# A list-scheduling kernel gets a planner with free slots, a rule against certain DVE and POOL instructions side by side, and a PE-clock term

## The chip, the cores and the metric

One core of a Trainium2 chip. The time is device microseconds of one execution. In the first measurement the kernel before takes 195.49 us (median of 4 runs, 195.04 to 196.26). The profile is one execution with the hardware profiler on; its span, from first to last instruction, is about 1.7 us shorter than the time of that same run (before: 193.5 and 195.17; after: 186.7 and 188.42). PE is TensorE, DVE VectorE, ACT ScalarE, POOL GpSimd, SP SyncE.

## The reference

A transformer block on 2048 tokens of width 448, modulated by one conditioning row. Attention has 16 heads of 28 and looks at 8 keys, every second token back; the MLP has 1792 hidden units.

```python
mod = (silu(c) @ w_mod).reshape(1, 6, 1, -1)      # sa, ca, ga, sb, cb, gb
h = layernorm(x) * (1 + ca) + sa
x = x + ga * attention(h, wqkv, wo)               # 8 keys, step 2 back
h = layernorm(x) * (1 + cb) + sb
x = x + gb * (gelu(layernorm(h) @ w1 + b1) @ w2 + b2)
```

## The kernel before

The kernel first collects tasks (an engine, an estimated duration, what it reads and writes), then a planner simulates the engines and emits the tasks in the order found. That order is fixed: each engine works through its own queue, and semaphores do the rest. So the planner's estimates are not the run time, but they decide who stands behind whom.

```python
QKE = "ADAADAAD"        # which engine copies each of 8 q/k groups from PSUM: A = ACT, D = DVE
ROOM = {"L": 2, "S": 4, "et": 3, "den": 4, "zh": 6, "yT": 3, "hm": 3, "vb": 3}
...
    def ps_one(shape, name, dtype=FP32):
        return Buf("S", lambda: ps_s.tile(shape, dtype, name=name, tag="s1"), name)   # 4 tiles in rotation
...
    def plan(self):         # [...] rank = longest tail to the end; then, in simulated time:
                for t in ready[e]:
                    [...]   # ready, and enough free tiles in its rooms
                    if best is None or (t.rank, -t.n) > (best.rank, -best.n):
                        best = t
```

The work: normalize 16 tiles of 128 tokens (statistics, z, transpose on PE, hT), project q and k in eight groups for 256 or 512 tokens at a time (pq), project v, then 17 blocks of attention (lt scores, their exponentials et, mask on DVE, pd and po sums, division oT), output projection (pw), second normalization (z2, h2, y), a DMA transposition to yT, and the MLP (p1, GELU, p2). The profile drops digits, so p1 and p2 both appear as `p`. PSUM is in two rooms: two tiles of two banks (lt, p1) and four of one bank (everything else). ACT loads a table between exponentials and GELU (1.28 us in the trace), so the blocks come in four phases.

Of the kernel before, what the change touches and what calls it, by code (L numbers as in the profile page):

```python
# [8 lines left out]
FP32 = mybir.dt.float32  # L9
BF16 = mybir.dt.bfloat16  # L10
ACT = mybir.ActivationFunctionType
# [20 lines left out]
QKE = "ADAADAAD"  # L32
# [7 lines left out]
FILL_UNTIL, FILL_SHARE = 12.0, 0.85  # L40
ROOM = {"L": 2, "S": 4, "et": 3, "den": 4, "zh": 6, "yT": 3, "hm": 3, "vb": 3}
SEM = 0.07
# [3 lines left out]
class Buf:  # L46


    def __init__(self, room, make, name=""):
        self.room, self.make, self.name, self.users, self._t = room, make, name, [], None  # L50

    @property
    def t(self):
        if self._t is None:
            self._t = self.make()
        return self._t


class Task:
    def __init__(self, n, eng, us, fn, bufs, rank_add, late):  # L60
        self.n, self.eng, self.us, self.fn, self.bufs = n, eng, us, fn, bufs
        self.name = f"{eng} {fn.__qualname__.split('.')[-1]}:{fn.__code__.co_firstlineno}"
        self.rank_add, self.late = rank_add, late
        self.before, self.after = {}, []
        self.rank = 0.0
        self.fill = 0


class Planner:
# [6 lines left out]
    def add(self, eng, us, fn, reads=(), writes=(), bufs=(), after=(), order_after=(), rank_add=0.0, late=0.0):  # L76
        t = Task(len(self.tasks), eng, us, fn, bufs, rank_add, late)
        for k in list(reads) + [b for b in bufs]:
            if k in self.writer:
                self._edge(self.writer[k], t, True)  # L80
        for k in writes:
            if k in self.writer:
                self._edge(self.writer[k], t, True)
            for r in self.readers.get(k, ()):
                self._edge(r, t, True)
            self.writer[k], self.readers[k] = t, []
        for k in reads:
            self.readers.setdefault(k, []).append(t)
        for b in bufs:
            b.users.append(t)  # L90
        for a in after:
            self._edge(a, t, True)
        for a in order_after:
            self._edge(a, t, False)
        self.tasks.append(t)
        return t
# [14 lines left out]
    def plan(self):  # L111
        for t in reversed(self.tasks):
            tail = 0.0
            for a in t.after:
                lag = (DRAIN[t.eng] + SEM + t.late) if a.before[t] else 0.0
                tail = max(tail, a.rank + lag)
            t.rank = t.us + tail + t.rank_add
        left = {t: len(t.before) for t in self.tasks}
# [5 lines left out]
        room = {r: list(range(n)) for r, n in ROOM.items()}  # L124
        held, users_left = set(), {}
        for t in self.tasks:
            for b in t.bufs:
                users_left[b] = len(b.users)
        free_at = {e: 0.0 for e in DRAIN}
        freeing = []  # L130
        order = []
        now = 0.0
        while len(order) < len(self.tasks):
            for f in sorted(freeing, key=lambda f: f[0]):
                if f[0] <= now:
                    room[f[1]].append(f[2])
            freeing = [f for f in freeing if f[0] > now]
            started = False
            for e in ("PE", "DVE", "ACT", "POOL", "SP"):
                if free_at[e] > now:  # L140
                    continue
                best = None
                for t in ready[e]:
                    if ready_at[t] > now:
                        continue
                    need = {}
                    for b in t.bufs:
                        if b not in held:
                            need[b.room] = need.get(b.room, 0) + 1
                    if any(len(room[r]) < n for r, n in need.items()):  # L150
                        continue
                    if best is None or (t.rank, -t.n) > (best.rank, -best.n):
                        best = t
                if best is None:
                    continue
                t = best
                if e == "PE" and now < FILL_UNTIL:
                    t.fill = int(max(0.0, now - free_at[e]) * FILL_SHARE / (0.43 if now < 6.0 else 0.215))
# [4 lines left out]
                for b in t.bufs:  # L163
                    if b not in held:
                        held.add(b)
                        b.slot = room[b.room].pop(0)
                end = now + t.us
                free_at[e] = end
                done = end + DRAIN[e] + t.late
                for b in t.bufs:  # L170
                    users_left[b] -= 1
                    if users_left[b] == 0:
                        freeing.append((done + SEM, b.room, b.slot))
# [10 lines left out]
            times = [v for v in free_at.values() if v > now] + [f[0] for f in freeing if f[0] > now]  # L184
            times += [ready_at[t] for e in ready for t in ready[e] if ready_at[t] > now]
            if not times:
                raise RuntimeError("no task can start: " + repr(room) + repr(
                    [(b.room, b.name, [(u.n, u.name) for u in b.users if u not in order]) for b in held if users_left[b]]))
            now = min(times)
        self.order = order  # L190
        self.span = max(free_at.values())

    def emit(self):
        for t in self.order:
            if t.fill:
                self.filler(t.fill)
            t.fn()
# [3 lines left out]
def kernel(  # L201
# [24 lines left out]
    ps_l = ctx.enter_context(tc.tile_pool(name="ps_l", bufs=ROOM["L"], space=bass.MemoryType.PSUM))  # L226
    ps_s = ctx.enter_context(tc.tile_pool(name="ps_s", bufs=ROOM["S"], space=bass.MemoryType.PSUM))
    wk = ctx.enter_context(tc.tile_pool(name="wk", bufs=3))
    hbm = ctx.enter_context(tc.tile_pool(name="hbm", bufs=1, space=bass.MemoryType.DRAM))

    def ps_big(shape, name):
        return Buf("L", lambda: ps_l.tile(shape, FP32, name=name, tag="l2"), name)

    def ps_one(shape, name, dtype=FP32):
        return Buf("S", lambda: ps_s.tile(shape, dtype, name=name, tag="s1"), name)

    def sb(room, shape, dtype, name):
        return Buf(room, lambda: wk.tile(shape, dtype, name=name, tag=room, bufs=ROOM[room]), name)
# [82 lines left out]
    add("ACT", 0.4, lambda: nc.scalar.dma_start(out=c_row[:, 0:D], in_=c), writes=["c_row"], late=2.0, rank_add=500)  # L321
# [10 lines left out]
    zero(0.6, lambda: hT[z_row, KT - 1, :], ["hT0"])  # L332
    zero(0.15, lambda: Wv[z_row, KT - 1, :], ["Wv0"])
# [11 lines left out]
    gate = None  # L345
    for i in range(2):
        gate = zero(0.8, lambda i=i: wmod2[i].t[z_row, KT - 1, :], [f"wmod0{i}"], [wmod2[i]], "POOL", 600 - 200 * i, [gate] if gate else [])
    add("DVE", 0.3, lambda: nc.vector.memset(wo_s[:], 0.0), writes=["wo"], rank_add=400)
# [17 lines left out]
    def pool(us, fn, writes, reads=(), rank_add=300, gated=True):  # L366
        add("POOL", us, fn, writes=writes, reads=reads, rank_add=rank_add, order_after=[gate] if gated else [])
# [73 lines left out]
    def normalize(dst, src, mv, which, b, reads, writes, bufs=()):  # L441
# [3 lines left out]
                   reads=list(reads) + [f"mv{id(mv)}_{b}", f"rs{which}_{b}"], writes=writes, bufs=bufs)  # L445
# [36 lines left out]
    def evac_h(kt, ptr, k, c0, n, eng, bs):  # L482
        kw = KW[kt]
# [36 lines left out]
    def spread(half, k0, k1, eng):  # L520
# [10 lines left out]
        if eng == "DVE":  # L531
            add("DVE", 0.08 + 0.134 * (k1 - k0), lambda: nc.vector.tensor_copy(out=o, in_=i()), reads=reads, bufs=[wqk_st], writes=[f"W{half}{k0}"])
# [6 lines left out]
    def front_qk(bs, engs):  # L539
        n, c0 = 128 * len(bs), tok_col(bs[0])  # L540
        for m in range(8):
            pq = ps_one([128, n], "pq")

            def mm(m=m, pq=pq):
                for kt in range(KT):
# [4 lines left out]
                        reads=[f"W{m // 4}0", f"W{m // 4}{KT - 1}", "hT0"]  # L550
                        + [f"h{kt}_{b}" for kt in range(KT) for b in bs], bufs=[pq]), pq)
# [9 lines left out]
    def mods():  # L561
# [19 lines left out]
        for i in range(2):  # L581
# [3 lines left out]
                reads=["ga"] + [f"wo{r}" for r in range(4)], writes=[f"wos{i}"])  # L585
# [3 lines left out]
    def w2_scale():  # L589
        for i in range(FT // 2):  # L590
            add("DVE", 0.55, lambda i=i: nc.vector.tensor_tensor(
                out=w2_s[:, 2 * i:2 * i + 2, :], in0=w2_s[:, 2 * i:2 * i + 2, :],
                in1=gb_bc.unsqueeze(1).to_broadcast([128, 2, D]), op=ALU.mult), reads=["gb"] + [f"w2l{k}" for k in (2 * i // 7, (2 * i + 1) // 7)], writes=[f"w2_{i}"])
# [4 lines left out]
    def attention(b, tbl, prev_w1):  # L598
# [3 lines left out]
        vbuf = Buf("vb", lambda: vbufs[vbuf.slot], "vb")  # L602
# [7 lines left out]
        P.wrote(add("PE", 0.76, vmm, reads=["wva", "wvb", "Wv0", "hT0"] + PADK + [f"h{kt}_{t}" for kt in range(KT) for t in tb], bufs=[pv, vbuf]), pv)  # L610
# [14 lines left out]
        lm = add("PE", 0.45, lmm, reads=PADK + [f"{s}{ft}_{t}" for s in "qk" for ft in range(4) for t in tb],  # L625
# [3 lines left out]
        for half in range(2):  # L629
# [10 lines left out]
            add("DVE", 0.57, msk, bufs=[et], reads=["mask"], writes=[(et, half)])  # L640
# [13 lines left out]
        P.wrote(add("PE", 0.62, dmm, reads=[(et, 0), (et, 1), "ones"], bufs=[et, vbuf, pd, po]), pd, po)  # L654
# [25 lines left out]
    def out_proj(t):  # L680
# [12 lines left out]
        if bi == 0:  # L693
# [8 lines left out]
                    reads=["g2"], bufs=[z2, h2]), h2)  # L702
        P.wrote(add("DVE", 0.31, lambda: nc.vector.tensor_tensor(out=h2.t[:], in0=h2.t[:], in1=sb_bc, op=ALU.add),
                    reads=["sb"], bufs=[h2]), h2)
# [76 lines left out]
    for half, engs in enumerate(SPREAD):  # L781
        spread(half, 0, KT - 1, engs[0])
        spread(half, KT - 1, KT, engs[1])
    front_qk([0, 1], "AAADAAAD")
# [6 lines left out]
    for pi, (blocks, tiles) in enumerate(phases):  # L791
        exps.clear()
        lt_mms.clear()
        for b in blocks:
            attention(b, tbl, prev_w1)
            if b == 0:
                front_ln([4, 5, 6, 7], False)
                front_qk([4, 5, 6, 7], QKE)
                mods()
            if b == 2:  # L800
                front_ln([8, 9, 10, 11], False)
                front_qk([8, 9, 10, 11], QKE)
                w2_scale()
            if b == 4:
                front_ln([12, 13, 14, 15], False)
                front_qk([12, 13, 14, 15], QKE)
# [44 lines left out]
```

## Time and profile before

| | before |
|---|---|
| time, median of 4 | 195.49 us |
| span of the profiled run | 193.5 us |
| PE work at full clock, counted from dense stretches | 164.5 us |
| of it ahead of the first MLP matmul (51.31 us) | 31.4 us |
| DVE busy from 20 to 46.47 us | all of it |

To read it, do not take PE's 93% busy for 93% useful. The fillers at the start (useless matmuls that are meant to bring the clock up) count as busy, and so do matmuls at half clock (the clock records show 0.50 from 47.52 to 50.93 us). How the work is counted instead, and the lines, are in the prediction.

### The profile page before, as it was taken

The numbers are of one execution on the slowest core, as the hardware profiler recorded it, in microseconds if no ns is written. First come the engines' busy times: TensorE is split into PE (matmuls) and PEld (weight loads), VectorE is DVE, ScalarE is ACT, GpSimd is POOL, SyncE is SP. The second block draws the span as 40 slices with busy tenths as digits, with TensorE's granted clock in tenths as the row PEclk, the third lists the DMA queues.
The fourth block names the chain that finished last, engine by engine and source line by source line (L and its number), as shares of the span: only waits on it lengthen the run. The fifth ranks groups of instructions, "written<-read, shape, count | busy, mean of one in ns | idle before, by whom it ended". The sixth has DMA issues, their size and how long they took to land.

```text
span 193.5 us, 4233 instructions
## 1 busy us (share of the span) xinstructions
PE 180.2 (93%) x1707; PEld 110.5 (57%) x1707; DVE 134.9 (70%) x352; ACT 114.4 (59%) x167; POOL 48.2 (25%) x90
## 2 busy tenths in 40 slices
PE   7799967994999999999999999999999989999991
PEld 2467543442584457687444574588547556756750
DVE  6998999999899778984758942980588677211102
ACT  3218998287469993876786725946774285232220
POOL 3391020255304125442004310440034134100000
PEclk9999999999799999999999999999999999999999
DMA  5999459801100110112001021003101130201101
GB/s 181 312 344 254 139 186 303 297 6 25 31 3 0 31 29 0 30 27 54 3 0 51 0 54 51 0 0 59 47 3 47 27 80 0 54 0 51 44 5 47
DMA packets 19000, 13.91 MB, mean 72 GB/s; under 512 B 9246, under 2 KB 18403, under 8 KB 18980
## 3 DMA queue, kind: packets, MB, share of 16 engines
q1 hardware_dynamic: 18978, 13.64, 25.1%
q8 instruction: 13, 0.21, 0.5%
q14 instruction: 7, 0.06, 0.1%
q10 hardware_dynamic: 2, 0.00, 0.0%
HBM read 9.70 MB, written 1.84 MB: 60 GB/s over the span
## 4 chain that ended last, share of the span: by engine, by line
PE 73%; DVE 11%; ACT 8%; DMA 3%; issue 2%; SPq 0%; DVEq 0%
PE p L736 25%; PE p L756 22%; PE pq L546 9%; PE pw L686 6%; PE pv L607 4%; ACT et L630 3%; DMA wm_st<-in_w_mod_dram 3%; DVE et L638 2%; PE lt L620 2%; PE pd L647 1%; PE po L651 1%; PE pwm L412 1%; ACT lden L657 1%; DVE oT L666 1%; DVE x_all L763 1%
## 5 line engine op out<-in xcount | busy, mean ns | idle before, releaser
L736 PE MATMUL p<-yT,w_s 128*128 128x256 bf16 x448 | 52.1, 272 | 0.2 <-ACT hm L743 0.2
L736 PEld LDWEIGHTS <-w_s 128*128 128x128 bf16 x448 | 43.4, 97 | 8.8 <-issue 0.8
L743 ACT ACTIVATE hm<-p 128x1024 bf16<-128x1024 f32 (+1 forms) x32 | 28.4, 915 | 32.2 <-PE p L736 32.2
L756 PE MATMUL p<-w_s,hm 128*128 128x448 bf16 x224 | 47.4, 353 | 0.0
L437 POOL TENSOR_TENSOR rs_all<-tv_all,neg_half 128x1 f32<-128x1 f32 (+1 forms) x35 | 21.7, 629 | 52.8 <-DVE tv_all L434 52.7
L630 ACT ACTIVATE et<-lt 128x976 bf16<-128x976 f32 x34 | 31.9, 996 | 4.3 <-PE lt L620 4.2
L763 DVE TENSOR_TENSOR x_all<-p,x1p_ring 128x448 bf16<-128x448 f32 x16 | 9.8, 619 | 34.2 <-PE p L756 34.2
L546 PE MATMUL pq<-hT,Wqk 128*128 128x512 bf16 (+3 forms) x160 | 31.9, 350 | 0.2 <-ACT mod_rows L573 0.2
L716 POOL TENSOR_TENSOR x1p_ring<-x_all,gbb_bc 128x448 f32<-128x448 bf16 x16 | 17.7, 1110 | 57.3 <-DVE x_all L690 37.3
L756 PEld LDWEIGHTS <-hm 128*128 128x128 bf16 x224 | 20.9, 98 | 17.7
L638 DVE TENSOR_TENSOR et<-et,mask 128x976 bf16<-128x976 bf16 x34 | 22.0, 654 | 6.0 <-ACT et L630 6.0
L546 PEld LDWEIGHTS <-Wqk 128*128 128x128 bf16 (+1 forms) x160 | 16.0, 103 | 13.9 <-issue 2.2
L419 DVE BATCH_NORM_STATS2 st_all<-x_all 128x6 f32<-128x448 bf16 x32 | 19.0, 614 | 0.1
L657 ACT ACTIVATE lden<-pd 128x488 f32<-128x488 f32 x17 | 9.9, 587 | 14.3 <-PE pd L647 14.3
L686 PE MATMUL pw<-wo_s,oT 128*128 128x448 bf16 x64 | 15.2, 367 | 1.9 <-DVE hT L487 1.1
L607 PE MATMUL pv<-Wv,hT 128*128 128x448 bf16 x68 | 15.2, 353 | 1.1 <-DVE oT L666 1.1
L558 ACT CAST qT<-pq 128x512 bf16<-128x512 f32 (+1 forms) x15 | 7.5, 507 | 9.4 <-PE pq L546 9.4
L611 ACT CAST vbuf<-pv 128x448 bf16<-128x448 f32 x17 | 9.1, 561 | 4.9 <-PE pv L607 4.8
L666 DVE SCALAR_TENSOR_TENSOR oT<-po,rden 128x484 bf16<-128x484 f32 x17 | 11.0, 654 | 1.2 <-ACT rden L659 1.2
L690 DVE TENSOR_TENSOR x_all<-pw,x_all 128x448 bf16<-128x448 f32 x16 | 9.9, 616 | 2.3 <-PE pw L686 2.3
L686 PEld LDWEIGHTS <-oT 128*128 128x128 bf16 x64 | 6.0, 100 | 8.1 <-DVE oT L666 1.4
L659 ACT ACTIVATE rden<-lden 128x488 f32<-128x488 f32 x17 | 10.4, 628 | 0.3
(82 smaller groups left out, 177.7 us busy)
## 6 DMA issues: line engine op xcount, KB each, us to landing
out_dram<-x_all SPq DMA_DIRECT2D x8, 224.0 KB, 2.0
w_s<-in_B_w_dram SPq DMA_DIRECT2D x2, 784.0 KB, 10.8
wmod<-in_w_mod_dram SPq DMA_DIRECT2D x2, 672.0 KB, 7.2
w_s<-in_B_w_dram SPq DMA_DIRECT2D x1, 1344.0 KB, 9.0
x_all<-in_A_x_dram SPq DMA_DIRECT2D x1, 896.0 KB, 8.8
wm_st<-in_w_mod_dram SPq DMA_DIRECT2D x1, 720.0 KB
wqk_st<-in_A_wqkv_dram SPq DMA_DIRECT2D x2, 339.0 KB, 5.5
x_all<-in_A_x_dram SPq DMA_DIRECT2D x2, 224.0 KB
```

The costliest lines, as they stand in the source:

```text
L419: add("DVE", 0.53, lambda: nc.vector.bn_stats(out=st_all[:, sl, :], in_=src()), reads=key, writes=[f"st{sl}"])
L437: lambda: nc.gpsimd.tensor_tensor(out=rs_all[:, which, b0:b0 + n], in0=tv_all[:, which, b0:b0 + n], in1=neg_half[:, 0:n], op=ALU.pow),
L546: nc.tensor.matmul(pq.t[:], lhsT=wqk_m(kt, m), rhs=hT[0:KE[kt], kt, c0:c0 + n], start=(kt == 0), stop=(kt == KT - 1))
L607: nc.tensor.matmul(pv.t[:], lhsT=hT[0:KE[kt], kt, k0:k0 + BK], rhs=Wv[0:KE[kt], kt, :], start=(kt == 0), stop=(kt == KT - 1))
L630: ex = add("ACT", 0.87, lambda half=half: nc.scalar.activation(out=et.t[:, 2 * half:2 * half + 2], in_=lts[half].t[:, :, 0:4 * EQ].rearran ...
L638: nc.vector.tensor_tensor(out=ev, in0=ev, in1=mask[:], op=ALU.mult)
L666: nc.vector.scalar_tensor_tensor(out=oT[:, :, o0:o0 + BQ], in0=po.t[:], scalar=DEN_SCALE, in1=rden.t[:, :, 0:BQ], op0=ALU.mult, op1=ALU.mult)
L686: nc.tensor.matmul(pw.t[:], lhsT=oT[:, ft, c0:c0 + 128], rhs=wo_s[:, ft, :], start=(ft == 0), stop=(ft == 3))
L716: nc.gpsimd.tensor_tensor(out=x1p_ring[:, t % NX1P, :], in0=x_all[:, t, :], in1=gbb2_bc[:], op=ALU.add)
L736: nc.tensor.matmul(p1.t[:, f, :], lhsT=w1_s[0:kp, kt, (fq + f) * 128:(fq + f + 1) * 128], rhs=yT.t[0:kp, kt, :], start=(kt == 0), stop=(kt ...
L743: gl = add("ACT", 0.18 + nf * 0.183, lambda fq=fq, nf=nf, p1=p1: nc.scalar.activation(out=hm.t[:, fq:fq + nf, :], in_=p1.t[:, 0:nf, :], fu ...
L756: nc.tensor.matmul(p2.t[:], lhsT=hm.t[:, ft, bi * 128:(bi + 1) * 128], rhs=w2_s[:, ft, :], start=(ft == 0), stop=(ft == FT - 1))
```

## The change

The intent is a better plan: each tile takes a slot chosen by the planner (any free one), the planner does not put certain DVE instructions beside POOL's (below the port or shared-port rule, after its names in the code; in the trace of before a normalize beside a 128x448 POOL instruction took 1.10 us and a multiply 1.23, others of these shapes 0.38), it repeats the plan with ranks from a backward pass, it charges for windows of 3.41 us in which PE would be busy less than 38%, lest its clock fall after them (both figures are settings in the code; no run here tests the 38%), and ranks get 2% of noise from a chosen seed. Some memsets move from DVE to POOL or go away, and ACT instead of DVE copies one more of every eight q/k groups in the three large sets (QKE).

```diff
-QKE = "ADAADAAD"
+START, NOISE, WINDOW = 0.8, 0.02, 3.4133
+PASSES = (44,)
+QKE = "AAADAAAD"
@@ planner, choice of the next task
+                shared = e in port and port["DVE" if e == "POOL" else "POOL"] > now
                 for t in ready[e]:
-                    if ready_at[t] > now:
+                    if ready_at[t] > now or (shared and t.port) or (best is not None and ...):
                         continue
[...]
-                        b.slot = room[b.room].pop(0)
+                        b.slot = min(range(ROOM[b.room]), key=lambda k: room[b.room][k])
[...]
+            for again in range(3):
+                order, span = self.forward()
+                cost = span + self.quiet(order)      # quiet: charge for windows with PE under 38%
+                [...]                                # the cheapest is kept
+                self.backward()
@@ tiles
-        return Buf("S", lambda: ps_s.tile(shape, dtype, name=name, tag="s1"), name)
+        return Buf("S", lambda k: ps.tile(shape, dtype, name=name, tag=f"S{k}"), name)
@@ memsets
-    zero(0.6, lambda: hT[z_row, KT - 1, :], ["hT0"])
-    zero(0.15, lambda: Wv[z_row, KT - 1, :], ["Wv0"])
+    zero(0.4, lambda: Wv[z_row, KT - 1, :], ["Wv0"], eng="POOL")
-    add("DVE", 0.3, lambda: nc.vector.memset(wo_s[:], 0.0), writes=["wo"], rank_add=400)
+    zero(1.6, lambda: wo_s[:], ["wo"], eng="POOL", rank=440)
@@ evac_h: the zero row comes out of the copy
-        kw = KW[kt]
+        kw = KE[kt]
```

> **What bounds the kernel now.** I read the page first, then busy times by stretch, then the chain of waits and the timelines of the stretch where TensorE (PE) is not full. From the page:
>
> ```profile
> PE 180.2 (93%) x1707; PEld 110.5 (57%) x1707; DVE 134.9 (70%) x352; ACT 114.4 (59%) x167; POOL 48.2 (25%) x90
> ...
> PE   7799967994999999999999999999999989999991
> DVE  6998999999899778984758942980588677211102
> PEclk9999999999799999999999999999999999999999
> ```
>
> PE is 93% busy, and each digit is a fortieth (4.84 us): PE has its holes in the first ten slices, where DVE is at 9. Busy PE includes fillers and half-speed matmuls, so I counted work instead. In dense stretches of the timeline a matmul takes, start to start: the MLP's first layer 110 ns (448 of them: 49.4 us), 448 columns 188.5 ns (224 of the second layer, 68 of V, 64 of the output projection: 67.1), 512 columns 216 ns and 256 columns 108 ns (the q/k projection: 27.6), the four-way packed attention scores 0.33 and their two sums 0.54 us for each of 17 blocks (14.8), transposes and modulation 5.6. Sum 164.5 us: the PE work in 193.5. Before the first MLP matmul at 51.31 us 31.4 us of it is done, so 19.9 us are lost there; from 51.31 to the last matmul's end at 189.2 pass 137.9 us for 133.2 of work, 4.7 lost; 4.3 us are the last add and store. Busy times by stretch (from:to, length, then PE, PEld, DVE, ACT, POOL busy with counts, PE clock, DMA share, GB/s) say the same:
>
> ```profile
> 20.00:30.00 10.00, 8.04 (x145) 5.09 (x144) 10.00 (x26) 9.63 (x19) 1.36 (x1) 1.00 0.48 172
> 30.00:40.00 10.00, 8.91 (x61) 4.15 (x60) 10.00 (x24) 5.11 (x9) 2.27 (x3) 1.00 0.83 255
> 40.00:46.47 6.47, 5.03 (x68) 2.78 (x67) 6.47 (x20) 6.01 (x11) 3.87 (x4) 1.00 0.01 1
> 46.47:51.31 4.84, 3.86 (x27) 1.57 (x27) 4.35 (x11) 2.59 (x4) 1.43 (x2) 0.65 0.29 56
> 51.31:100.00 48.69, 48.18 (x519) 30.84 (x521) 39.28 (x101) 37.06 (x51) 13.18 (x18) 1.00 0.09 18
> 100.00:158.10 58.10, 57.40 (x546) 34.18 (x539) 38.02 (x96) 35.64 (x49) 13.33 (x19) 1.00 0.13 34
> ```
>
> DVE is the bound from 20 to 46 us, PE from 51 on. The chain of waits (start, us, what) shows the hand-over: DVE work without a gap to the second normalized tile, its DMA transposition, then the MLP:
>
> ```profile
> 45.33 1.42 DVE ybuf L442 x2
> ...
> 50.16 1.31 PE pq L546 x4
> 51.47 6.17 PE p L736 x56
> ```
>
> The four q/k matmuls at 50.16 take 1.31 us where 0.86 is usual: the clock (0.65 in that stretch) had fallen after a 1.5 us wait for a mask.
>
> [...] a normalize takes about 0.31 us otherwise (start to start), and here 1.03 and, with the multiply, 1.15, each ending as the POOL instruction does:
>
> ```profile
> 38.88 1.11 POOL L586 TENSOR_TENSOR gbb_bc<-mod_bc,b_bc 128x448 f32<-128x448 bf16 x1
> 40.07 1.26 POOL L716 TENSOR_TENSOR x1p_ring<-x_all,gbb_bc 128x448 f32<-128x448 bf16 x1
> ```
> ```profile
> 39.02 1.10 DVE L442 TENSOR_SCALAR z<-x_all,mv,rs_all 128x448 bf16<-128x448 bf16 x1
> 40.35 1.23 DVE L701 TENSOR_TENSOR h<-z,mod_bc 128x448 bf16<-128x448 bf16 x1
> ```
>
> [...]
>
> **The change part by part.** The mathematics and all 1,690 or so real matmuls stay (the same 164.5 us); only order, buffer slots and a few constants move. I read the order of both kernels, engine by engine.
>
> *Front.* The zero row of hT (0.92), Wv's (0.24) and half of wo_s (0.81) leave DVE's start; the row now comes out of ACT's copy, 65 partitions instead of 64, at no cost. They lay before data arrived: the first matmul on real weights waits for the modulation weights, landed at 6.88 us, unchanged. After it DVE now does first what the q/k projection waits for. Before:
>
> ```profile
> 8.48 0.15 DVE L474 COPY mod_col<-ps_col 128x4 f32<-128x4 f32 x1
> 8.54 0.15 DVE L476 TENSOR_SCALAR mod_col<-ps_col 128x4 f32<-128x4 f32 x1
> 8.61 0.62 DVE L532 COPY Wqk<-wqk_st 65x512 bf16<-65x512 bf16 x1
> 9.15 0.39 DVE L487 TENSOR_SCALAR hT<-ptr,mod_col 128x256 bf16<-128x256 bf16 x1
> 9.47 1.16 DVE L532 COPY Wqk<-wqk_st 128x1536 bf16<-128x1536 bf16 x1
> 10.55 0.39 DVE L487 TENSOR_SCALAR hT<-ptr,mod_col 128x256 bf16<-128x256 bf16 x1
> ```
>
> The second hT copy now stands behind one 0.54 us weight copy, not two and a POOL memset (1.08 instead of about 0.63). From 8.61, or 8.8 when the transposition is done: 0.33 + 0.54 + 0.33 = 10.0, start of q/k about 10.2 instead of 11.09: 0.9 us gained, unless K weights (0.5 + 0.63 later, 11.15) cost 0.2 back. Mask and pads on POOL now wait for these copies (about 11) and, from their 5 us of instructions, are done near 16, just before the first use.
>
> *First block.* Its scores are now ahead of the transposes of tiles 2 and 3. By the same sums its masks are at about 16.7 and 17.8 on DVE instead of 19.11 and 20.35; its exponentials come before, so the row of modulations leaves ACT near 20.7, not 22.8, and the weights scaled by it and the MLP loads, all behind it, gain 2 us.
>
> *20 to 51 us, the main part.* DVE's instructions between its first wait and the end of the second normalized tile sum to 37.7 us before, 41.3 after, from these durations: the new order does tiles 8 to 11's hT (1.2), two of their q/k copies (1.2) and a third output tile ahead of it, while q/k copies of DVE fall from three to two of eight (0.60 each on DVE, 0.50 on ACT, which had 4.9 us free from 30 to 40). Walking the queue with its waits I get the second tile at 48.2 us (before 46.7), and the MLP 2.8 later (half of what the transposition and landing took before, since the first tile's goes earlier): about 51. So the MLP does not start earlier. But PE has 38.2 us of work before it instead of 31.4: all eight q/k groups of tiles 8 to 11 (6.9 us) fill the 40 to 51 us in which 4.9 us were lost and the clock fell. PE's side: third output projection at 41.7 us (behind the fourth block's division), then 0.75 + 8 x 0.86 + 0.54 + 0.75 = 8.9, to 50.6, at most 51.1 with waits for the four single-bank PSUM slots. Lost until the MLP: 51.1 - 38.2 = 12.9 instead of 19.9: **7.0 us**, of which 0.9 is the front.
>
> *After.* PE has 126.4 us left. ACT's run between the two GELU stretches (8 exponentials at 0.87, copies, logarithms, two table loads) sums to 19.6 us, and PE has 26.1 us of work until it needs the two-bank slots back: no new hole. I keep 4.7 lost and 4.3 of tail. Span 51.1 + 126.4 + 4.7 + 4.3 = 186.5, and time is 1.85 over the span (195.35 against 193.5): 188.3. I add 0.7 for port collisions left in my walk (it has none; before had 2.4 us of them up to 46.5): 189.0.
>
> **Rivals.** *Only the front counts*: if PE's earlier q/k groups wait for PSUM, because their evacuations queue on ACT and DVE, the lost time only moves, and 194 to 195 results. For: DVE has 3.6 us more to do ahead of the MLP. Against: six of eight evacuations are ACT's, and one takes 0.50 where the group takes 0.86. *A new bound later*: greedy slots or noisy ranks (2%, one seed) put an exponential or mask late, PE idles and the clock falls, as at 45 us; 191 to 193. For: the planner's durations differ from the trace (memsets, ACT copies). Against: 51 to 158 us has only 1.2 us of PE not busy, with the same rooms. *More than I think*: if later stretches also improve and the collisions vanish, 186. Slower would take an early-data surprise, such as the wo_s memset on POOL holding up ident; ident is needed at about 8 us and is due before 4.
>
> **Range and chances.** The walk is good to perhaps 2 us in the middle and 1.5 after: 186.0 to 192.4 for 8 in 10. The 2% line is 191.4 us; I give faster 0.85, same 0.13, slower 0.02.
>
> **What would show it.** Right: q/k starts near 10.2; first mask near 16.7; MLP starts at 50 to 52 with tiles 8 to 11's q/k all ahead of it; PE clock 1.00 from 40 to 51; DVE without 1 us normalizes before it; the rest no longer than 136. Wrong: an MLP start past 54, a clock drop in a new place, or waits of PE for ACT copies between 20 and 50 us.

## The result

The kernel after takes 188.19 us (median of 4, 187.83 to 189.25), before 195.49. Ratios here are the mean time of one kernel's fast runs over that of the other's in the same rounds, so not quite the ratio of the medians: 0.963, with a 95% interval of 0.958 to 0.968.

From the page of the profile after (busy us and share by engine, then the slices):

```profile
PE 176.1 (94%) x1709; PEld 107.9 (58%) x1709; DVE 131.2 (70%) x346; ACT 116.9 (63%) x170; POOL 49.3 (26%) x93
...
PE   4997888999999999999999999999999999999991
DVE  3798799999994999787805799798259878211102
PEclk9999999999999999999999999999999999999999
```

PE's share has risen by one point only, though 6.8 us of span are gone. Its busy time fell from 180.2 to 176.1 for the same matmuls and two fillers more, in part because in the records its clock is 1.00 from 6.84 us to the last matmul, where that of before is 0.50 for 3.41 us. The sixth, seventh and tenth slices of PE, 6, 7 and 4 before, are 8, 8 and 9. Busy times by stretch, for the same stretches as in the prediction:

```profile
20.00:30.00 10.00, 8.99 (x112) 5.85 (x111) 8.77 (x23) 7.66 (x15) 0.00 (x0) 1.00 0.75 229
30.00:40.00 10.00, 9.40 (x94) 4.24 (x83) 10.00 (x26) 7.33 (x14) 2.56 (x3) 1.00 0.71 191
40.00:46.47 6.47, 6.04 (x55) 3.01 (x54) 6.47 (x21) 5.29 (x9) 4.19 (x5) 1.00 0.11 22
46.47:51.31 4.84, 4.84 (x41) 2.18 (x40) 4.84 (x15) 3.10 (x6) 2.41 (x3) 1.00 0.14 27
```

DVE (third figure after the length) is as full as before from 30 us on. PE, the first, went from 5.03 to 6.04 in 40 to 46.47 us and from 3.86 to 4.84 in the next stretch, at a clock of 1.00 instead of 0.65. The chain that ended last shows with what:

```profile
44.29 5.36 PE pq L615 x24
...
50.19 1.84 PE pq L615 x8
52.03 0.76 PE pv L676 x4
52.79 6.17 PE p L805 x56
```

These 32 matmuls are the eight q/k groups of tiles 8 to 11. Before, one of the eight ran just ahead of the MLP (at 49.95 us) and seven after it had begun; with one v projection these seven are the 6.8 us that moved. The MLP (`p L805`) begins 1.3 us later than before, but with 38.2 us of PE work behind it instead of 31.4. PE's timelines, before and after:

```profile
51.31 6.33 PE L736 MATMUL p<-yT,w_s 128*128 128x256 bf16 x56
```
```profile
52.63 6.33 PE L805 MATMUL p<-yT,w_s 128*128 128x256 bf16 x56
```

The sum of the gain in span ("lost" is time less work, so it holds the clock's falls too): before the MLP, 19.9 us lost became 52.63 - 38.16 = 14.5, so 5.4; from there to the last matmul's end at 182.35 pass 129.7 us for 126.4 of work, 3.3 lost instead of 4.7, so 1.4; the tail is the same. Together 6.8 = 193.5 - 186.7.

### The profile page after: what moved, and what is told of

Its sections match the earlier page's. It is cut to its first block, busy times and chain, and to the rows that moved or that the text cites. A ratio compares the mean times of both kernels' runs of the same rounds, so it can differ in the third digit from the quotient of the medians.

```text
span 186.7 us, 4230 instructions
## 1 busy us (share of the span) xinstructions
PE 176.1 (94%) x1709; PEld 107.9 (58%) x1709; DVE 131.2 (70%) x346; ACT 116.9 (63%) x170; POOL 49.3 (26%) x93
## 4 chain that ended last, share of the span: by engine, by line
PE 81%; DVE 8%; ACT 4%; DMA 4%; issue 1%; DVEq 0%; ACTq 0%
PE p L805 26%; PE p L825 23%; PE pq L615 12%; PE pw L755 6%; PE pv L676 5%; PE pd L716 3%; DMA mod_bc<-mod_hbm 3%; PE lt L689 2%; DVE st_all L488 2%; PE po L720 2%; ACT hT L560 1%; PE pwm L481 1%; DVE et L707 1%; DMA mod_hbm<-mod_rows 1%; ACT hm L812 1%; ACT et L699 1%
## 5 line engine op out<-in xcount | busy, mean ns | idle before, releaser
L805 PE MATMUL p<-yT,w_s 128*128 128x256 bf16 x448 | 52.3, 272 | 0.5 <-ACT hm L812 0.5
L805 PEld LDWEIGHTS <-w_s 128*128 128x128 bf16 x448 | 43.5, 97 | 9.3 <-issue 1.1
L825 PE MATMUL p<-w_s,hm 128*128 128x448 bf16 x224 | 46.7, 353 | 0.0
L506 POOL TENSOR_TENSOR rs_all<-tv_all,neg_half 128x1 f32<-128x1 f32 (+1 forms) x35 | 22.2, 640 | 58.5 <-DVE tv_all L503 58.4
L615 PE MATMUL pq<-hT,Wqk 128*128 128x512 bf16 (+3 forms) x160 | 30.9, 337 | 2.0 <-ACT mod_rows L642 0.8
L707 DVE TENSOR_TENSOR et<-et,mask 128x976 bf16<-128x976 bf16 x34 | 23.0, 684 | 11.6 <-ACT et L699 11.3
L785 POOL TENSOR_TENSOR x1p_ring<-x_all,gbb_bc 128x448 f32<-128x448 bf16 x16 | 17.0, 1060 | 44.8 <-DVE x_all L759 26.4
L615 PEld LDWEIGHTS <-Wqk 128*128 128x128 bf16 (+1 forms) x160 | 14.8, 97 | 14.4 <-issue 3.2
L755 PE MATMUL pw<-wo_s,oT 128*128 128x448 bf16 x64 | 14.3, 353 | 0.1
L676 PEld LDWEIGHTS <-hT 128*128 128x128 bf16 x68 | 6.4, 98 | 6.1 <-issue 0.7
```

Of the source, the lines that this page charges most:

```text
L506: lambda: nc.gpsimd.tensor_tensor(out=rs_all[:, which, b0:b0 + n], in0=tv_all[:, which, b0:b0 + n], in1=neg_half[:, 0:n], op=ALU.pow),
L615: nc.tensor.matmul(pq.t[:], lhsT=wqk_m(kt, m), rhs=hT[0:KE[kt], kt, c0:c0 + n], start=(kt == 0), stop=(kt == KT - 1))
L676: nc.tensor.matmul(pv.t[:], lhsT=hT[0:KE[kt], kt, k0:k0 + BK], rhs=Wv[0:KE[kt], kt, :], start=(kt == 0), stop=(kt == KT - 1))
L707: nc.vector.tensor_tensor(out=ev, in0=ev, in1=mask[:], op=ALU.mult)
L755: nc.tensor.matmul(pw.t[:], lhsT=oT[:, ft, c0:c0 + 128], rhs=wo_s[:, ft, :], start=(ft == 0), stop=(ft == 3))
L785: nc.gpsimd.tensor_tensor(out=x1p_ring[:, t % NX1P, :], in0=x_all[:, t, :], in1=gbb2_bc[:], op=ALU.add)
```

## The experiments

Twelve kernels ran, all correct. In the first call runs of before spread widely on that chip (194.67 to 199.04), so its ratios have wide intervals and I compare times as well; there warm, which keeps the order of after, took 188.08. Where an edit makes the planner plan anew, the whole order can change; this is said each time.

### hold: q/k groups of tiles 8 to 11 kept behind the first MLP group

```diff
+            if bs[0] == 8:
+                held_qk.append(pqt)
[...]
+    for t in held_qk:
+        P._edge(first_w1[0], t, False)
     P.plan()
```

> The new planner and everything else kept, but the eight q/k groups of tiles 8 to 11 (6.9 us of PE work) may not start before the first MLP matmul group has been issued. My theory (the gain is PE work pulled ahead into the stretch that DVE bounds): the MLP again starts near 50 to 52 us, with only about 32 us of PE work done before it, so about 19 us are lost there instead of 14.5; the time goes to 192.5 to 195.5. Rival (free slots, port model and front are the gain, the pulled-ahead groups only fill a hole that closes by itself): the MLP starts about 6 us earlier, near 47, and the time stays within 188 to 190.

198.19 us (197.74 to 199.44), ratio to before 1.014 (1.003 to 1.024). The gain is gone and more. Busy times by stretch of this run:

```profile
40.00:46.47 6.47, 5.98 (x72) 3.19 (x71) 6.44 (x25) 5.57 (x10) 5.04 (x7) 1.00 0.00 1
46.47:51.31 4.84, 2.69 (x28) 1.13 (x27) 4.77 (x10) 4.78 (x8) 3.68 (x4) 1.00 0.14 29
```

PE is busy for 2.69 us of the 4.84, as it waits from 49.3 us for an oT division; then four matmuls take 1.67 us, where four of this shape take 0.92 at 46.61 in the same run:

```profile
51.78 1.67 PE L760 MATMUL pw<-wo_s,oT 128*128 128x448 bf16 x4 [2.48 <-DVE oT L740]
```

The MLP starts at 53.25 with 32.0 us of work done: 21.2 lost. So, against the rival, the MLP did not move earlier when PE had less to do before it; it could not, since the transposition of its second tile landed only at 52.64. The time overshot my 192.5 to 195.5. The plan is a new one, it lost clock twice (3.41 us each, from 31.13 and 51.61 us; the mean clock is 0.83 from 30 to 40 us and 0.96 from 51.31 to 100) and 2.1 us more after the MLP began than before did; and before itself took 197.58 in this call. That excess is not explained further.

### rot: the order of after, with rotating tiles

```diff
-        return Buf("S", lambda k: ps.tile(shape, dtype, name=name, tag=f"S{k}"), name)
+        return Buf("S", lambda k: ps.tile(shape, dtype, name=name, tag="S", bufs=ROOM["S"]), name)
```

(and the same for the other rooms; PE's order was compared and is the same)

> The order of the kernel after on every engine, unchanged, but the tiles of one pool rotate as before, instead of each taking the slot that was planned. 64 of the 136 single-bank PSUM tiles and 16 of the 67 double-bank ones then sit in another slot than the plan's. Theory that the order is the gain: at most 1 us slower, 188 to 189.3. Rival that free slots are what makes this order run: PE waits for the oldest tile (an attention sum held until its division) in a dozen places before 50 us, and the time goes to 190 to 194, with waits of q/k groups for oT or x_all in the trace.

188.79 us (188.45 to 189.29), ratio 0.965 (0.958 to 0.973). Taking the slots back costs 0.6 us or less: three measurements in the order of after gave 188.19, 188.57 (again) and 188.08 (warm, on this chip). One new wait is to be seen among q/k groups, in PE's timeline (start, length, what, and in brackets the idle time before it with its releaser):

```profile
47.52 2.76 PE L615 MATMUL pq<-hT,Wqk 128*128 128x512 bf16 x12 [0.29 <-DVE x_all L759]
```

The tile there had to wait for an older one's addition, and the MLP starts at 53.26 instead of 52.63. I had counted a dozen places where rotation would make PE wait by the plan's times; nearly all of them are not to be seen.

### b_slots: the order of before, with planned slots

```diff
-        return Buf("S", lambda: ps_s.tile(shape, dtype, name=name, tag="s1"), name)
+        return Buf("S", lambda k: ps_s.tile(shape, dtype, name=name, tag=f"S{k}"), name)
```

> The kernel before in its own order on every engine (checked to be the same, instruction for instruction), but every PSUM and SBUF tile sits in the slot that its planner found free, instead of rotating. Theory (at a fixed order the slots matter little, as rotating cost the kernel after 0.6 us): 0 to 1 us faster than before. Rival (rotation is what starved PE before the MLP): 3 us or more faster, with the MLP starting near 48.

195.30 us, ratio 1.000 (0.997 to 1.003). The slots alone are worth nothing in the old order. With rot this shows that at a fixed order slots are worth little, one way or the other.

### b_front: the memset moves alone, in before

```diff
-    zero(0.6, lambda: hT[z_row, KT - 1, :], ["hT0"])
-    zero(0.15, lambda: Wv[z_row, KT - 1, :], ["Wv0"])
+    zero(0.4, lambda: Wv[z_row, KT - 1, :], ["Wv0"], eng="POOL")
-    add("DVE", 0.3, lambda: nc.vector.memset(wo_s[:], 0.0), writes=["wo"], rank_add=400)
+    zero(1.6, lambda: wo_s[:], ["wo"], eng="POOL", rank=440)
[...]   # kw = KE[kt], no wait on "hT0"
```

> The kernel before with the moved memsets alone: zero row of hT out of ACT's 65-row copy, Wv's row and wo_s zeroed on POOL; old planner, old split of q/k copies. Theory (the front is mostly hidden behind later waits, as moving q/k by half a microsecond did not move the end): within 1 us of before. Rival (the front is worth the 0.9 us of my prediction or more): q/k starts 0.9 us or more earlier and the time falls by 1 to 2 us.

196.55 us, ratio 1.003 (1.000 to 1.006). PE's order stays the same. Three DVE memsets less, q/k 0.3 us earlier (10.80 against 11.09), and no gain. So it tests 0.3 us of the front (the time up to the first q/k matmul), not the 0.9 of the prediction, which counted on a new order of the copies too.

### warm: the fillers' memset first, one filler less

```diff
+        self.order.sort(key=lambda p: p[0].n != 0)
+        self.order = [(t, min(f, 2) if t.n == self.c_cols.n else f) for t, f in self.order]
```

> The order of the kernel after, with two edits: the memset of the filler's operand is the first on DVE (it was the seventh, so the fillers began at 2.77 us), and one filler less ahead of the matmuls on c, which then begin near 3.1 us instead of 5.02. If the front is on the path that sets the end (theory): the first weight matmuls begin near 6.9 us (DMA landing) instead of 7.52, q/k near 9.7 instead of 10.02, and 0.3 to 0.7 us come off the time. Rival (the front is hidden, since DVE bounds the stretch up to the MLP and waits for x tiles at 22 us): less than 0.2 us.

188.08 us (187.79 to 192.02), ratio 0.961 (0.955 to 0.968; the run of 192.02 counts as slow): no difference from after, as the rival said. The matmuls on c did come at 3.50 instead of 5.02 and the weight matmuls waited only for their DMA. But q/k started later, at 10.56 instead of 10.02. The timelines of POOL and DVE in this run show the reason:

```profile
7.95 0.84 POOL L388 MEMSET wmod<- 1x896 bf16 x1 [3.59 <-PE ps_col L541]
```
```profile
8.00 1.33 DVE L604 COPY Wqk<-wqk_st 128x1536 bf16<-128x1536 bf16 x1 [1.33 <-DMA wqk_st<-in_A_wqkv_dram]
```

The earlier matmuls freed a buffer earlier, so POOL's memset began 50 ns ahead of DVE's weight copy, which then took 1.33 us instead of 0.68 (in after the copy began at 8.11 us, the memset at 8.53). So here an instruction off the path set when one on it was done. And although q/k was 0.54 us later, the MLP was only 0.12 us later (52.75): the front is mostly hidden, in this direction too.

### b_qke: the new split of q/k copies alone, in before

```diff
-QKE = "ADAADAAD"
+QKE = "AAADAAAD"
```

> The kernel before with two instead of three of eight q/k copies on DVE for the three large groups. Theory (DVE bounds 20 to 46 us): one copy of 0.60 us off DVE before the MLP, 0.3 to 1 us faster, more only if the order happens to change. Rival (the split alone brings the q/k groups forward): 3 us or more faster.

194.75 us over 20 runs, ratio 0.992 (0.990 to 0.995), with a new plan. That is 1.5 us by the ratio, above the 0.3 to 1 expected; but 7 of its 20 runs count as slow and are left out of it, and over all runs the difference is 1.2 us. Six runs show a mean clock of 0.998 or more and take 193.4 us on average, so a part of it is the clock; PE's work ahead of the MLP is 31.3 us, unchanged. These six also bound the clock: with no fall of it, but only 31.3 us of work ahead, the kernel is still 4.9 us above after's runs without a fall (188.5, on other chips).

### noport: the planner without the shared-port rule

```diff
-                    if ready_at[t] > now or (shared and t.port) or (best is not None and ...):
+                    if ready_at[t] > now or (best is not None and ...):
```

> The planner of after without the shared-port rule: DVE and POOL instructions may be planned side by side; same seed. Theory (the port rule removes 2 to 3 us of DVE stalls, of which only those before the MLP count): normalizes and multiplies of about 1 us appear again before 52 us, MLP start 1 to 2 us later, time 189.5 to 191.5. Rival (the port rule does nothing, or order noise outweighs it): 187.5 to 189.

190.85 us (190.53 to 192.46), ratio 0.977 (0.968 to 0.986), with a new plan. Collisions are back, for instance (POOL, then DVE):

```profile
45.06 1.39 POOL L785 TENSOR_TENSOR x1p_ring<-x_all,gbb_bc 128x448 f32<-128x448 bf16 x1
```
```profile
45.48 1.23 DVE L770 TENSOR_TENSOR h<-z,mod_bc 128x448 bf16<-128x448 bf16 x1
```

In the profiled run, the slowest of the four (192.46), the MLP starts at 54.47 with 36.3 us of work done. The collisions before it that I find come to about 1.1 us of DVE time, while 3.6 us more are lost than in after. The clock fell once in this run (3.41 us from 30.36 us; the mean is 0.83 from 30 to 40), which the profiled run of after does not show; how the rest divides between that and the other order is open. The 2.7 us are the worth of the rule together with the order it led to.

### seed0: the new planner without noise

```diff
-PASSES = (44,)
+PASSES = (0,)
```

> The kernel after without the 2% noise on the ranks (port rule, backward passes and everything else kept). PE has 34.7 us of work ahead of the first MLP matmul in this order, against 38.2 in after and 31.4 in before. Theory (the pulled-ahead work is the gain, and the seed is what found an order with all of it): about half of the gain goes, 190.5 to 193. Rival (the rules make the gain, the noise is polish): 188 to 189.5.

192.69 us (190.56 to 193.09), ratio 0.986 (0.979 to 0.992). With all rules and no chosen seed, about two fifths of the gain is there (by the interval, a fifth to almost three fifths). The MLP starts at 52.93, with 34.7 us of work ahead.

### seed878 and split10: other plans; again: the kernel after once more

Some 1,800 seeds of the unchanged planner and 400 each of four other splits were compared by the planner's own estimate (by my count; the search is not on record); two of the best ran, beside a repetition of after.

```diff
 # seed878                       # split10
-PASSES = (44,)                 -PASSES = (44,)
+PASSES = (878,)                +PASSES = (10,)
                                -QKE = "AAADAAAD"
                                +QKE = "AADAADAA"
```

> The kernel after with another seed for the noise; 38.9 us of PE work stand ahead of the first MLP matmul, against 38.2. By the theory a little faster than after: 186.8 to 188.2. If the planner's order counts less than chance on the chip: 188 to 190.

> The kernel after with another seed and with q and k copies three to five between the engines in other places (third and sixth of eight on DVE instead of fourth and eighth); 38.6 us of PE work ahead of the first MLP matmul. By the theory, as the planner packs it best of all that I tried: 185.5 to 187.5. Otherwise: 188 to 190.

> The kernel after once more, on the same chip as the others of this call, as their base: 187.8 to 188.8, mean clock 0.99 or more in every run, where runs of before spread from 194.4 to 198.5 with clocks from 0.991 down to 0.965.

seed878 188.51 us, ratio 0.969 (0.965 to 0.972); split10 188.08, ratio 0.967 (0.963 to 0.971); again 188.57, ratio 0.970 (0.967 to 0.973). The three cannot be told apart, so I claim no version that beats the kernel after; both other plans missed the range that the theory gave them, and lie in that of its rival. A little more work ahead of the MLP (38.9 and 38.6 us) gave nothing more: the MLP of seed878 starts at 53.92, so its work is bought with as much time.

### b_fill: useless matmuls to keep the clock, in before (inconclusive)

```diff
+                if b == 4 and r == 1:
+                    for _ in range(7):
+                        nc.tensor.matmul(po.t[:].rearrange("p f c -> p (f c)")[:, 0:D], lhsT=ident[:], rhs=Wv[0:128, 0, :],
+                                         start=True, stop=True)
```

> The kernel before, its order unchanged, with seven extra matmuls (448 columns, 1.3 us of full-array work whose result is overwritten) in the fifth block's sums, where PE waited 1.53 us for a mask and the clock then fell. If the clock is a large part of what after gained (rival: no useful work had to move): PE clock 1.00 from 40 to 52 us, MLP start 1.0 to 1.5 us earlier, time 1 to 1.7 us shorter. If the gain is work pulled ahead (theory): the clock may hold, but the MLP still waits for the second tile's transposition, so less than 0.7 us, on average over the runs.

197.82 us (196.61 to 198.97), ratio 1.015 (1.011 to 1.020). It was meant to separate the clock from the useful work and does not, for it brought a new wait. PE's timeline:

```profile
46.70 0.38 PE L647 MATMUL pd<-et,ones_k 128*32 128x488 bf16 x2
49.13 2.77 PE L651 MATMUL po<-Wv,ident 128*128 128x448 bf16 x7 [2.05 <-DVE oT L670]
```

The fillers write into the PSUM tile of po, which in before is first needed when the mask has come. Now PE asks for it earlier and waits 2.05 us for the block before to be divided; then the seven take 2.77 us, 396 ns each, where 448 columns take 188.5 in before's dense stretches (mean clock 0.72 from 46.47 to 51.31). No run gave the fillers a tile of their own.

## Why the prediction was right

**What bounds the kernel** was right: DVE to about 46 us, PE after it. The ledger of lost PE time adds up to both spans by its making, since "lost" is a difference; it locates the gain but does not prove a cause. One reading was loose: the chain shown in the prediction does not run through the DMA transposition. Its omitted pieces go from the tile to a mask, a division, PE's sums, output projection and q/k (46.75 to 51.47 us). But the transposition is hardly off it: by the trace's record of its landing it ended at 51.01, and the MLP began at 51.31.

**The main part.** The mechanism was as predicted: the MLP does not start earlier, it starts with more done. hold is the direct test. Side by side, from the profiled runs (work from the order, at the spacings of the prediction; "tile landed" is the end of the transposition of the MLP's second tile; lost is start less work):

| kernel | work ahead of the MLP | tile landed | MLP starts | lost | this run | median |
|---|---|---|---|---|---|---|
| before | 31.4 | 51.01 | 51.31 | 19.9 | 195.17 | 195.49 |
| b_slots | 31.4 | 52.60 | 52.88 | 21.5 | 196.77 | 195.30 |
| b_qke | 31.3 | 51.81 | 51.95 | 20.7 | 196.29 (slow) | 194.75 |
| hold | 32.0 | 52.64 | 53.25 | 21.2 | 198.54 | 198.19 |
| seed0 | 34.7 | 52.28 | 52.93 | 18.2 | 192.34 | 192.69 |
| noport | 36.3 | 53.93 | 54.47 | 18.1 | 192.46 | 190.85 |
| after | 38.2 | 51.88 | 52.63 | 14.5 | 188.42 | 188.19 |
| rot | 38.2 | 52.05 | 53.26 | 15.1 | 189.07 | 188.79 |
| split10 | 38.6 | 52.45 | 52.59 | 14.0 | 187.51 | 188.08 |
| seed878 | 38.9 | 53.67 | 53.92 | 15.0 | 188.49 | 188.51 |

Over 7.6 us of difference in work the start moves by 3.2 us and does not follow the work. It follows the landing, 0.1 to 0.8 us behind it (1.2 in rot): the tile comes off DVE, so less work on PE could not have brought the MLP forward by more than that.

The term was over-sized: 7.0 us predicted, 5.4 measured, as the MLP started at 52.63 instead of 51.1. Two steps were off. "PE's side: third output projection at 41.7 us" ran at 43.08, behind the fourth block's division (41.49 to 42.12) and a v projection; and the q/k groups began only at 44.29, because they waited for ACT's half of hT, copied at 42.80 to 44.24 behind two exponentials (41.05 to 42.91). The prediction counts no such wait. "I get the second tile at 48.2 us" was the other: it was ready at 49.45 and landed at 51.88, so even with PE on time the MLP would have begun at least 0.8 us later than predicted. Two of the prediction's own signs say the same: the start is outside its "50 to 52", and PE did wait for ACT copies between 20 and 50 us, a sign of being wrong, though only by 0.44 and 0.28 us.

**The front.** "0.9 us gained" was right as an event (q/k at 10.02 instead of 11.09, predicted 10.2) and wrong as a term of the sum. b_front (0.3 us earlier) and warm (0.54 later) show that so much there does not reach the end. In the ledger it looks like a gain, since the time lost before q/k is smaller; that later waits would have taken up the whole 0.9 is likely, but not shown. One thing I did not see coming: the fillers began at 2.77 us, behind other memsets, and held the matmuls on c back from 3.11 to 5.02 us. The front still gained, partly as the collision of a POOL memset with a weight copy was gone: in before the second 128x1536 copy took 1.16 us beside a memset that had begun 0.33 us earlier, and the first 0.69; in after one of the two stands ahead of q/k and takes 0.68. The zero row's copy on ACT cost next to nothing: 64x512 took 775 ns in before, 65x512 775 in after (64x256 552, 65x256 573). Another part of the front was, as an estimate from the spacing of matmuls, the clock: in the profiled run of before the first q/k matmuls are about 210 ns apart until 13.4 us, where the clock records begin, 32 of them in 4.64 us (the profile's PEclk line shows 9 there all the same); in that of after they take 3.54 us, 110 ns each from the start. I had read those 4.64 us in the profile without asking why. b_front's profiled run has its clock records from 10.59 us, its q/k matmuls are 110 ns apart from their start at 10.80, and it still starts the MLP at 52.15; but its clock fell for 3.41 us at 31.07 (mean 0.83 from 30 to 40, where before's is 1.00), so this does not settle what the early clock is worth.

**First block.** Masks at 16.30 us (predicted 16.7), modulation row out of ACT at 20.40 (predicted 20.7, before 22.82).

**After the MLP's start.** I kept 4.7 us lost; 3.3 were, a gain of 1.4 I had left out. No new hole came, as the sum of ACT's run had said.

**Collisions of DVE and POOL.** The 0.7 us that I added for collisions was right in kind and somewhat small: ahead of the second tile a DVE statistics step (128x4) took 0.93 us beside POOL (0.17 elsewhere), a normalize 0.73 (0.38 elsewhere), together 1.1 us. That is most of the 1.25 us by which the tile came late. The multiply, over the whole kernel, by groups of lines before and after (count, busy us, mean ns, idle before):

```profile
L701 DVE TENSOR_TENSOR h<-z,mod_bc 128x448 bf16<-128x448 bf16 x16 | 7.3, 459 | 0.2
```
```profile
L770 DVE TENSOR_TENSOR h<-z,mod_bc 128x448 bf16<-128x448 bf16 x16 | 5.9, 382 | 0.1
```

So the sum came out near (189.0 predicted, 188.19 measured) partly by luck: of a predicted gain in span of 6.3 us (7.0 less 0.7 for collisions) 5.4 came before the MLP, and 1.4 that the prediction had left out came after it. The 1.85 us that it set between span and time (a median against another run's span) is 1.7.

**The rivals.** "Only the front counts" falls with hold and with the order of the work (b_front tests a part of the front alone). "A new bound later" did not come in this order. seed0 lands in its range with 192.69, but for another reason: it loses 18.2 us before the MLP and some 3.6 after it. "More than I think" is not seen. A rival that the prediction did not name is the split of the q/k copies: alone, in the old planner, it gave 1.2 to 1.5 us (b_qke), without any work moved ahead of the MLP.

**The clock, a part left open.** The prediction counted the clock's fall within the lost time and gave it no term. In the profiled run of before PE's clock is 0.50 for 3.41 us from 47.52 us on. In the 3.41 us ahead of that, from 44.11, PE was busy for 1.08 us, with transposes and small packed sums, and its longest wait was 1.53 us; that is 32% busy, but no run tests what share would have kept the clock. In the profiled run of after the clock does not fall between 6.84 us and the last matmul. The falls whose records are quoted here, in before, hold, noport and b_front, last 3.41 us each. One takes some 0.009 off the mean clock of a run (3.41 x 0.50 of 193.5 us; that run's mean is 0.991), so as an estimate the mean counts them. Over the three calls, runs of before with one such window by that count average 195.0 us (16 runs), with two 195.6 (36), with four 197.4 (16): about 0.8 us for each. Runs of after have none in 8 of 10 counted in the same way (188.5 us on average). As an estimate from these numbers, some 1 to 1.5 of the 7.3 us may be the clock. In the profiled run of before the fall can have delayed the MLP by 0.3 us at most, since its tile landed only at 51.01. No run separates it in the order of before: b_fill was to, and failed. But the six runs of b_qke without a fall leave 4.9 us to after, so the clock is not the main part.

## What to carry to other kernels

When one engine bounds a stretch and another bounds the rest, look for work of the second that can run inside the stretch; the start of the next stage need not move for the time to fall. Count work at the spacing of dense stretches, not busy time, and the sum of lost time will tell where a gain must come from, but a gain at the front is only one if no later wait takes it up. A planned order is one draw: the rules alone gave about two fifths of this gain, the chosen seed the rest; of the parts tried alone in the old kernel neither the slots nor the memsets gave anything, and the split of the q/k copies gave 1.2 to 1.5 us.
